# The second half of the first token tile's first row block, loaded by SP's queue instead of ScalarE's

## The chip, the cores and the metric

The kernel runs on one core of a Trainium2 chip. A core has five engines with instruction streams of their own: TensorE (PE in the profile, with its weight loads as PEld), VectorE (DVE), ScalarE (ACT), GpSimd (POOL) and SyncE (SP). SP does no arithmetic here; it issues nearly all DMA transfers. ScalarE issues two of them, at the very start. The transfers of both are carried out by the core's 16 DMA engines.

The metric is the device time of one execution, in microseconds (us), as the median of several runs. The profile is that of one execution.

## The reference

Two branches work on the same tokens `x` (2048 tokens of 448 numbers, float32), and a gate mixes them:

```python
x = A_x
g = _sigmoid((x * gate_w).sum(-1, keepdims=True))
a = _A_ref(x, A_wqkv, A_wo)           # local attention: 16 heads of 28, 8 keys, every second position back
b = _B_ref(x, B_w1, B_b1, B_w2, B_b2) # relu(x @ w1 + b1) ** 2 @ w2 + b2, with 1792 hidden numbers
return g * a + (1 - g) * b
```

In the attention branch `x @ wqkv` gives queries, keys and values. Each query meets the keys at its own position and at 2, 4, ... 14 positions before it. The result is multiplied by `wo`.

## The kernel before, in words

All matrix products are made to float32 accuracy from parts: a matrix is split into a high part (rounded to the type that TensorE multiplies) and a low part (what is left), and a product is high x high, high x low and low x high. So each weight and each token block needs a copy by ScalarE (the high part) and a subtraction by VectorE (the low part) before TensorE can use it.

The 2048 tokens are four chunks of 512 (`CH`), stored transposed: 448 rows of features, 512 columns of tokens. The 448 rows are three row blocks of 128 (k = 0, 1, 2) and a last one of 64, which stands twice, so that two matmuls of 64 rows can run side by side. A chunk's first work is queries, keys and values: for each of its four token tiles of 128 tokens a matmul per row block and part. After all four chunks follow the dense branch's products and the output product, while the attention's elementwise work runs on GpSimd, VectorE and ScalarE.

From line 811 on the order of the work on ScalarE, VectorE and SP comes from a planner (`Plan`), which keeps an estimate of each engine's time. Everything around this change stands before that, in the opening (lines 763 to 808), whose order is written out by hand:

- 18 matmuls on zeros (line 771) keep TensorE busy until data comes.
- ScalarE's queue loads the first token block (k = 0) of chunk 0 in two halves of 256 columns (line 778). The first half holds token tiles 0 and 1, the second half tiles 2 and 3.
- SP's queue loads, for k = 0, 1, 2, the weights of the queries (line 781; 128 rows of 450 numbers, 448 of the queries and two of the gate), with the tokens of the row block behind them (line 786). For k = 0 there are only weights, since the tokens come by ScalarE's queue. For k = 3 the weights are two pieces of 64 rows (line 784). Then follow the weights of keys and values (lines 790 and 793), and later the next chunks' tokens (line 617).
- ScalarE copies the high part of each row block's weights (line 796) and of its tokens (line 799); for the first half it is VectorE that copies (line 801). VectorE subtracts for the low parts: weights on line 803, tokens on line 804. Both engines work strictly in this order.

TensorE's first real work is `qkv_first`, on line 402: for row block 0 first tiles 0 and 1, then tiles 2 and 3, each with three parts; then row blocks 1 and 2 with all four tiles:

```python
for k in range(3):
    todo = [full(x, q[i], i, 0, (k,)) for i in four]
    for some in ((0, 1), (2, 3)) if k == 0 else (four,):
        for j in range(3):
            for i in some:
                acc, a, w, *_ = todo[i][j]
                nc.tensor.matmul(acc.pt[:, :NQ], a, w, start=k == j == 0, stop=False)
```

That makes 3 x 4 x 3 = 36 matmuls. Behind them come the paired matmuls of line 315 (`side_by_side`), which make up the rest of the kernel but for its last stretch.

Of the kernel before, what the change touches and what calls it, by code (L numbers as in the profile page):

```python
# [22 lines left out]
CH = 512  # L23
# [155 lines left out]
def gated_mix_kernel(ctx: ExitStack, tc: tile.TileContext, xT, wqkv, w1, w2, wo, b1, b2, out):  # L179
    nc = tc.nc  # L180
# [593 lines left out]
    raws = [rawp.tile([P, 4, 512], F32, tag="raw", name="wqraw0")]  # L774
    rx = rawp.tile([P, 4, 512], F32, tag="raw", name="xraw0")
    halves = slice(0, 256), slice(256, CH)
    for cols in halves:
        nc.scalar.dma_start(rx[:, 0, cols], xT[0, :, 0, cols])
    for k in range(4):
        if k < 3:  # L780
            nc.sync.dma_start(raws[0][:, k, :NQ], wqkv[0, :, k])
        else:
            for b, rows in ((0, slice(0, 64)), (1, slice(64, P))):
                nc.sync.dma_start(raws[0][rows, k, :NQ], wqkv[b, rows, k])
        if k:
            nc.sync.dma_start(rx[:, k], xT[0, :, k])
    for b, tag in ((1, "k"), (2, "v")):
        raw = attp.tile([P, 3, D], F32, tag=tag, name=f"wqraw{b}")
        for k in range(3):
# [516 lines left out]
```

## Time and profile before

| | us |
|---|---|
| median of 3 runs | 416.2 (415.88 to 416.37) |
| the profiled execution | 415.95 |
| its span, from the first to the last instruction | 414.1 |
| busy in the span: TensorE | 408.6 |
| busy: VectorE / ScalarE / GpSimd | 258.6 / 206.0 / 265.8 |

The profile's times count from the first instruction of the span. A row of a timeline gives the start, the length, the engine (with a q for its sequencer, as where it issues a DMA), the line, the operation, what it writes and reads, how many such instructions were merged, and in brackets the idle time of the engine before it with what ended it. Where several were merged, the length reaches from the first one's start to the last one's end. Matmuls overlap, so a matmul's length is longer than the distance to the next; the distance of the starts is the pace. In the names, `wqraw` holds raw weights of queries, keys and values, `xraw` raw tokens, `wqh` and `wql` the weights' high and low parts, `x` the parts of the tokens.

### The profile page before, as it was taken

The page shows a single profiled execution, that of the slowest core. Times are in us where ns is not written, and L with a number is a line of the kernel's source. Part 1 is how long each engine was busy: PE and PEld are TensorE (multiplying, and loading weights), DVE is VectorE, ACT ScalarE, POOL GpSimd, SP SyncE. Part 2 cuts the span into 40 slices and gives each one's busy share as a digit, 9 for nine tenths or more (in the row PEclk, how much of TensorE's full clock was granted, in tenths as well). Part 3 has the DMA queues.
Part 4 walks back from the last instruction along what each step waited for, and adds up shares of the span by engine and source line. Part 5 has one row for each costly group of instructions (what it writes and reads, how often), then busy time and mean ns, then how long its engine had stood idle before and what let it go on. Part 6 is the DMA issues. An engine that isn't in the chain of part 4 may idle for free.

```text
span 414.1 us, 9249 instructions
## 1 busy us (share of the span) xinstructions
PE 408.6 (99%) x3828; PEld 404.2 (98%) x3828; DVE 258.6 (62%) x346; ACT 206.0 (50%) x501; POOL 265.8 (64%) x165
## 2 busy tenths in 40 slices
PE   8999999999999999999999999999999999999996
PEld 7999999999999999999999999999999999999995
DVE  4514523484386768777656899786767586593453
ACT  5746766242464665444555435345615344346730
POOL 0000000876969999889999897999998975950000
PEclk9999999999999999999999999999999999999999
DMA  7999999845164433544203669663626022068404
GB/s 242 377 346 295 398 378 372 309 156 205 46 215 188 150 106 132 208 161 152 82 4 127 223 149 310 218 162 64 218 91 232 4 90 85 22 158 157 112 2 178
DMA packets 64555, 73.75 MB, mean 178 GB/s; under 512 B 32321, under 2 KB 57345, under 8 KB 64129
## 3 DMA queue, kind: packets, MB, share of 16 engines
q1 hardware_dynamic: 64224, 72.90, 53.5%
q8 instruction: 30, 0.49, 0.5%
q10 hardware_dynamic: 288, 0.26, 0.2%
q14 instruction: 13, 0.10, 0.1%
HBM read 45.71 MB, written 28.25 MB: 179 GB/s over the span
## 4 chain that ended last, share of the span: by engine, by line
PE 98%; DMA 1%; DVE 0%; ACT 0%; issue 0%
PE b L315 32%; PE h L315 32%; PE qkv L315 23%; PE a L315 7%; PE qkv L402 2%; PE a L1096 1%; DMA wqraw<-wqkv 1%; DVE bt_b L987 0%; ACT wqh L796 0%
## 5 line engine op out<-in xcount | busy, mean ns | idle before, releaser
L504 POOL TENSOR_TENSOR pp<-q,k 128x896 f32<-128x896 f32 x64 | 135.1, 2152 | 86.9 <-DMA k<-k_d 78.4
L516 POOL TENSOR_TENSOR pp<-lg,v 128x896 f32<-128x896 f32 x64 | 118.9, 1962 | 4.3 <-DVE lg L508 2.6
L315 PE MATMUL qkv<-wqh,x 64*128 64x448 f32 (+1 forms) x528 | 91.6, 362 | 0.0
L757 DVE TENSOR_TENSOR h<-h,h 128x512 fp32r<-128x512 f32 x56 | 38.7, 691 | 67.2 <-ACT h L756 66.8
L315 PE MATMUL b<-w2ah,h 64*128 64x448 f32 x448 | 78.8, 359 | 0.0
L315 PE MATMUL b<-w2bh,h 64*128 64x448 f32 x448 | 78.7, 359 | 0.0
L508 DVE TENSOR_REDUCE lg<-pp 128x32 f32<-128x896 f32 x64 | 67.5, 1077 | 14.0 <-POOL pp L504 14.0
L315 PE MATMUL qkv<-wql,x 64*128 64x448 f32 (+1 forms) x264 | 75.2, 362 | 0.0
L315 PEld LDWEIGHTS qkv<-wqh,x 64*128 64x128 f32 x528 | 74.0, 184 | 0.3
L526 DVE TENSOR_REDUCE o<-pp 128x112 f32<-128x896 f32 x64 | 67.2, 1069 | 3.1 <-POOL pp L516 3.1
L315 PEld LDWEIGHTS b<-w2ah,h 64*128 64x128 f32 x448 | 63.8, 184 | 0.0
L315 PEld LDWEIGHTS b<-w2bh,h 64*128 64x128 f32 x448 | 62.9, 184 | 0.2
L315 PE MATMUL b<-w2al,h 64*128 64x448 f32 x224 | 63.1, 358 | 0.0
L315 PE MATMUL b<-w2bl,h 64*128 64x448 f32 x224 | 62.3, 358 | 0.0
L753 ACT ACTIVATE h<-h,b1z 128x512 f32<-128x512 f32 x56 | 36.7, 656 | 41.1 <-PE h L315 41.1
L315 PEld LDWEIGHTS qkv<-wql,x 64*128 64x128 f32 x264 | 44.7, 184 | 0.2
L315 PEld LDWEIGHTS b<-w2al,h 64*128 64x128 f32 x224 | 38.4, 184 | 0.0
L315 PEld LDWEIGHTS b<-w2bl,h 64*128 64x128 f32 x224 | 37.7, 184 | 0.1
L315 PE MATMUL h<-x,w1h 64*128 64x512 f32 x168 | 35.7, 386 | 0.0
L315 PE MATMUL h<-x0b,w1h 64*128 64x512 f32 x168 | 35.6, 386 | 0.0
L337 ACT ACTIVATE st<-qkv 128x448 f32<-128x448 f32 x48 | 24.4, 541 | 21.8 <-PE qkv L315 15.8
L755 ACT ACTIVATE h<-h 128x512 fp32r<-128x512 f32 x56 | 33.5, 598 | 1.5
(132 smaller groups left out, 855.6 us busy)
## 6 DMA issues: line engine op xcount, KB each, us to landing
k<-k_d SPq DMA_DIRECT2D x8, 840.0 KB, 6.1
v<-v_d SPq DMA_DIRECT2D x8, 840.0 KB, 4.7
x_d<-x SPq DMA_DIRECT2D x12, 512.0 KB, 6.4
q_d<-st SPq DMA_DIRECT2D x8, 448.0 KB, 4.8
k_d<-st SPq DMA_DIRECT2D x8, 448.0 KB, 4.7
v_d<-st SPq DMA_DIRECT2D x8, 448.0 KB, 5.5
q<-q_d SPq DMA_DIRECT2D x8, 448.0 KB, 3.3
o_d<-o SPq DMA_DIRECT2D x16, 224.0 KB, 2.2
```

The lines of the kernel that those rows point to most:

```text
L315: nc.tensor.matmul(acc.pt[:, :acc.n], a[rows], w[rows], start=acc.todo == acc.all, stop=acc.todo == 1)
L337: nc.scalar.activation(st[0][:, :, t % 2], pt[:, :D].rearrange("p (g c) -> p g c", g=G), AF.Copy)
L402: nc.tensor.matmul(acc.pt[:, :NQ], a, w, start=k == j == 0, stop=False)
L504: nc.gpsimd.tensor_mul(pr.rearrange("p (w c) -> p w c", w=W), q[:, s:s + 1].to_broadcast([P, W, C]), k[:, s:s + W])
L508: nc.vector.tensor_reduce(lgs[i][:, s], pr.rearrange("p (w h d) -> p w h d", w=W, h=HG), axis=AX.X, op=ALU.add)
L516: nc.gpsimd.tensor_mul(pr.rearrange("p (h d w) -> p w h d", h=HG, w=W), lgs[i][:, s][:, :, :, None].to_broadcast([P, W, HG, DH]), vs[i][:, ...
L526: nc.vector.tensor_reduce(o_t[par, s][:, g * C:(g + 1) * C], pr.rearrange("p (c w) -> p c w", w=W), axis=AX.X, op=ALU.add)
L753: a = add(ACT, 656.0, lambda pt=pt, r=r: nc.scalar.activation(pt, pt, AF.Relu, bias=b1t[:, f + r:f + r + 1]), ready, bias_job[0], prio=NEXT)
L755: b = add(ACT, 600.0, lambda pt=pt, hh=hh: nc.scalar.activation(hh, pt, AF.Square), a, prio=NEXT)
L757: low = add(DVE, 690.0, lambda pt=pt, hh=hh, hl=hl: nc.vector.tensor_sub(hl, pt, f32(hh)), a, prio=NEXT)
L1096: nc.tensor.matmul(acc.pt[:, :D], a, w, start=False, stop=acc.todo == 1)
```

## The change

For row block 0, the second half of the tokens (columns 256 to 511) is no longer loaded by ScalarE's queue. SP's queue loads it, right behind the first weights and ahead of the second weights. The first half stays with ScalarE's queue. The loads, their sizes and their destinations are the same; the number of DMA instructions is the same, one less on ScalarE and one more on SP. Nothing is changed in the copies, the subtractions or the matmuls.

```diff
     halves = slice(0, 256), slice(256, CH)
-    for cols in halves:
-        nc.scalar.dma_start(rx[:, 0, cols], xT[0, :, 0, cols])
+    nc.scalar.dma_start(rx[:, 0, halves[0]], xT[0, :, 0, halves[0]])
     for k in range(4):
         if k < 3:
             nc.sync.dma_start(raws[0][:, k, :NQ], wqkv[0, :, k])
         else:
             for b, rows in ((0, slice(0, 64)), (1, slice(64, P))):
                 nc.sync.dma_start(raws[0][rows, k, :NQ], wqkv[b, rows, k])
-        if k:
-            nc.sync.dma_start(rx[:, k], xT[0, :, k])
+        cols = slice(0, CH) if k else halves[1]
+        nc.sync.dma_start(rx[:, k, cols], xT[0, :, k, cols])
```

## The prediction

> **What bounds the kernel now.** I read the page first, then the chain of work that ended last, then the opening by engine. On the page:
>
> ```profile
> span 414.1 us, 9249 instructions
> PE 98%; DMA 1%; DVE 0%; ACT 0%; issue 0%
> ```
>
> The second line gives shares of the chain: TensorE carries 98% of it. The chain's first 14 us (start, length, what) and the busy times of one long stretch (TensorE, its weight loads, VectorE, ScalarE, GpSimd, clock, DMA share, GB/s):
>
> ```profile
> 0.74 3.60 DMA wqraw<-wqkv
> ...
> 4.37 0.59 ACT wqh L796
> ...
> 5.00 7.99 PE qkv L402 x36
> ...
> 13.00:406.00 393.00, 393.00 (x3756) 390.87 (x3756) 248.85 (x327) 198.75 (x489) 264.99 (x152) 1.00 0.53 175
> ```
>
> From 13 us to 406 us TensorE is busy for 393.00 of 393.00 us at clock 1.00. So whatever the opening gains or loses is handed on to the end one for one, and no change to the opening's loads can do more than move the moment at which this stretch begins. Before it stand 36 matmuls of line 402 in 7.99 us. How many of those us are waiting is seen in the timelines of TensorE (PE), and of its weight loads (PEld):
>
> ```profile
> 5.66 0.68 PE L402 MATMUL qkv<-wql,x 128*128 128x450 f32 x2
> 6.18 1.21 PE L402 MATMUL qkv<-wqh,x 128*128 128x450 f32 x4
> 7.23 0.56 PE L402 MATMUL qkv<-wql,x 128*128 128x450 f32 x2
> 7.63 1.36 PE L402 MATMUL qkv<-wqh,x 128*128 128x450 f32 x6
> 6.70 0.30 PEld L402 LDWEIGHTS qkv<-wqh,x 128*128 128x128 f32 x2 [0.33 <-ACT x L799]
> ```
>
> From 7.23 to 7.63 two matmuls start 0.20 us apart; that is the undisturbed pace. 36 of them need 7.20 us, so the stage holds 7.99 - 7.20 = 0.79 us of stalls. One of these belongs to the change: between 6.18 and 7.23 four matmuls took 1.05 us instead of 0.80. Its weight load, at 6.70, waited for ScalarE's copy on line 799, which is the copy of the second half of the tokens. **That stall costs 1.05 - 0.80 = 0.25 us**, the wait and the slow restart after it together. The other stalls (0.54 us) stand before it, at the first weights and their low part.
>
> Why that copy is late, ScalarE and VectorE show (the bracket is the idle time before and what ended it):
>
> ```profile
> 1.67 1.28 ACT L796 ACT_TABLE_LOAD   x1 [1.67 <-PEq L1298]
> 4.37 0.58 ACT L796 ACTIVATE wqh<-wqraw 128x450 fp32r<-128x450 f32 x1 [1.42 <-DMA wqraw<-wqkv]
> 6.23 0.42 ACT L799 ACTIVATE x<-xraw 128x256 fp32r<-128x256 f32 x1 [1.28 <-DMA xraw<-xT]
> 6.55 0.56 ACT L796 ACTIVATE wqh<-wqraw 128x450 fp32r<-128x450 f32 x1
> 7.02 0.61 ACT L799 ACTIVATE x<-xraw 128x512 fp32r<-128x512 f32 x1
> 7.65 0.58 ACT L796 ACTIVATE wqh<-wqraw 128x450 fp32r<-128x450 f32 x1
> 8.58 0.63 ACT L799 ACTIVATE x<-xraw 128x512 fp32r<-128x512 f32 x1 [0.34 <-DMA xraw<-xT]
> 4.54 0.29 DVE L801 CAST x<-xraw 128x256 fp32r<-128x256 f32 x1 [3.54 <-DMA xraw<-xT]
> 4.98 0.63 DVE L803 TENSOR_TENSOR wql<-wqraw,wqh 128x450 fp32r<-128x450 f32 x1
> 5.52 0.42 DVE L804 TENSOR_TENSOR x<-xraw,x 128x256 fp32r<-128x256 f32 x1
> ```
>
> ScalarE stood idle for 1.28 us, until the second half landed at about 6.2. The first half had landed at 4.5, the first weights at 4.34.
>
> **The change, part by part.** The issues of the two queues, SP's waits, and the landings of two later loads (the last number, from issue):
>
> ```profile
> 0.74 0.90 ACTq L778 DMA_DIRECT2D xraw<-xT  x2
> 0.74 0.86 SPq L781 DMA_DIRECT2D wqraw<-wqkv  x2
> 1.65 0.43 SPq L786 DMA_DIRECT2D xraw<-xT  x1
> 2.13 0.43 SPq L781 DMA_DIRECT2D wqraw<-wqkv  x1
> 3.08 1.94 SPq L784 DMA_DIRECT2D wqraw<-wqkv  x2
> 6.22 3.21 SPq L790 DMA_DIRECT2D wqraw<-wqkv  x6
> SPq L784 <- DMA xraw<-xT: 0.9, 1, 0.9
> wqraw<-wqkv SPq DMA_DIRECT2D x1, 225.0 KB, 4.8
> xraw<-xT SPq DMA_DIRECT2D x1, 256.0 KB, 5.0
> ```
>
> *ScalarE loses one DMA issue* (0.90/2 = 0.45 us). Its table load begins about 0.45 earlier, at 1.2. Worth nothing: 1.42 us of idle time follow it, ended by the first weights.
>
> *SP gains one issue*, behind the first weights and ahead of six others of its own: second weights, second tokens, third weights, third tokens and the two pieces on line 784. Each is issued some 0.43 later, up to the second piece. That one waits 0.9 us for the first half (it comes to issue at 4.53, beside VectorE's cast of that half at 4.54), so the delay ends there: 0.43 of the 0.9 us is used up, and everything behind is not later. Whether the delay of the others shows depends on whether the transfers wait for their issue. The packets (q1 is SP's queue, q10 ScalarE's; shares are of 16 engines) in 1.7 to 3.5 us, 3.5 to 5 us, and the total line of 5 to 6.2 us:
>
> ```profile
> DMA packets 258, 0.35 MB, mean 195 GB/s; under 512 B 16, under 2 KB 258, under 8 KB 258
> ...
> q1 hardware_dynamic: 143, 0.24, 54.7%
> q10 hardware_dynamic: 115, 0.11, 21.4%
> q1 hardware_dynamic: 188, 0.31, 58.0%
> q10 hardware_dynamic: 169, 0.15, 38.9%
> DMA packets 266, 0.45 MB, mean 375 GB/s; under 512 B 31, under 2 KB 152, under 8 KB 266
> ```
>
> The two queues take turns, packet by packet (143 against 115, then 188 against 169), and from 3.5 us the engines are 97% taken. A load of 128 rows is 128 packets (0.24 MB in 143 packets is 1.7 KB each, near a row of 450 floats), so eight for each of 16 engines. By 3.5 us the first weights are through and the first half nearly (115 of 128), so the second weights were issued at about 1.2 and moved from about 3.5: over 2 us of cover for 0.43 us of delay. Costed at nothing; without the cover it would be 0.43 us on each landing.
>
> *The first half and the first weights* hold the first place of their queues before and after, and share the engines as before. Their landings, and so the first matmul at 5.00, I leave where they are. Bounds: nothing; or 0.12 us earlier, as ScalarE's copy could begin sooner but VectorE's cast ends at 4.54 + 0.29 = 4.83, against 4.95 of the copy.
>
> *The second half* took its turns on q10 against the second weights (4.8 us from 1.19, landing 5.99) and landed at 6.2, after them. On SP's queue it stands ahead of them, and q10 is empty once the first half is through. A packet of q10 costs 38.9% x 1.5 us x 16 / 169 = 0.055 us, so eight take 0.44 us: landing at 4.52 (just ahead of VectorE's cast of the first half) + 0.44, about **5.0**. Bounds: with the first half (4.5), or not at all earlier (6.2). I take 5.0, since the packet price comes from this very load. ScalarE is free at 4.95, so its copy runs from 5.0 to 5.45, beside idle time. TensorE wants the result at 6.38 + 0.20 = 6.58 at the new pace; the cover is 1.1 us, and even a landing at 6.1 would do. VectorE's low part of the half follows at 5.52 + 0.42 = 5.94 and is done at 6.4; it is wanted four matmuls after 6.58, at 7.38. **The stall of 0.25 us goes.**
>
> *The second weights* now come after the half. The same bytes are through by then as before at 6.2, so they land between 5.8 and 6.2; ScalarE's copy, which before ran at 6.55 behind the half's, starts at 6.0 to 6.2. The second tokens (1.65 + 5.0, landing near 6.65) have the same bytes ahead of them as before. Their copy starts at 6.7 instead of 7.02 and ends at 7.3.
>
> *What is late next.* The second block's first matmul, at 7.63 + 2 x 0.20 = 8.03 before, is wanted at 7.78: 0.47 us after the 7.3. The third weights (copy at 7.65) and third tokens (copy 8.58 to 9.21, set by their landing) are wanted 12 matmuls later, at 10.18. Nothing there takes the place of the stall.
>
> *The loads of line 790* wait for the landings, one by one: the first, at 6.22, stands right behind the half's landing. It can go out about half a us earlier, once the third tokens are issued behind the wait of line 784, and the next ones up to 0.5 us earlier. They queue behind all that the opening needs.
>
> **The sum:** -0.25 us, all else nothing. The profiled execution took 415.95 us round its span of 414.1; the median of the runs is 416.2. So 415.70 for such an execution, and **415.95** against the median.
>
> A rule that speaks against this: the Trainium skill, "DMA: Bandwidth & Descriptors", section "Issuing engines are not separate DMA queues", says that DMAs from several engines run on the same 16 engines and interleave, and that issuing from several at once saves only the sequencer's issue time. By that alone the half would land no sooner, and SP would pay the 0.43 us. The same page, section "Queues, rings and completion order", has the engines take turns between queues and each ring go in order; by that the half comes before the second weights, and the sum is the -0.25 above; by the first it would be nothing, the first rival below. The turns of q1 and q10 above agree with the latter; no run here yet shows which decides for the landing.
>
> **The rivals.**
>
> *The half lands no sooner.* It shares the engines anyhow, and they were full until 6.2. The stall stays where it is: 416.2. For it speaks the 97%; against it, that the second weights landed ahead of the half (5.99) and would now have to stand behind it in their own queue.
>
> *The second block becomes late (slower).* If the half's time adds to q1 in full and the delay of issue as well, the second tokens land 0.44 + 0.43 later, at 7.55; their copy ends at 7.58 + 0.61 = 8.19, and the second block starts at about 8.24 instead of 8.03: +0.2, 416.4. It decides from a landing at about 7.1 on (7.78 less 0.61 and the handing over), and turns the gain to a loss beyond 7.35. Against it: the engines are full, so q10's empty turns go to q1.
>
> *The first matmul moves too (faster).* From 1.7 to 3.5 us the engines moved 195 GB/s, later 375. If the second ScalarE load has to do with that, the first weights and half (225 KB and 128 x 256 floats, 361 thousand bytes) could land up to 361/195 - 361/375 = 1.85 - 0.96 = 0.9 us earlier. Then 0.9 + 0.25 is gained at the most, 415.1; half of it gives 415.5. Against it: the half's packets come only after the first half's, so they can't slow what stands before them.
>
> **How the numbers follow.** Forecast 0.63, half no sooner 0.14, second block late 0.11, first matmul earlier 0.12. About 0.2% (0.83 us) is what a measurement of this kernel can tell from no change; its three runs lie 0.49 us apart. The forecast and the first two rivals lie within that. Of the third, most of the upper end is beyond it: faster 0.10, with a little for the forecast with a larger gain, 0.13 in all. Slower by that much wants the second tokens at 8.2, 1.5 us later: 0.04. Range: 415.95 with the runs' half spread (0.25) is 415.7 to 416.2; it reaches to the slow rival with its spread above (416.7) and below to half of the fast rival's gain, with most of the spread (415.3).
>
> **What would show it.** In the changed profile: one issue on line 778; ScalarE's 128x256 copy near 5.0, not 6.23; four matmuls from about 6.18 in 0.80 us; the second block from 7.78; the long stretch from 12.7. Wrong if the copy still waits until 6, if a weight load waits at the second block, or if the first matmul isn't at 5.0.

## The result, and the profile after

| | us |
|---|---|
| after: median of 12 runs | 416.72 (416.29 to 417.49) |
| before, in the same comparison: median of 12 runs | 415.88 (415.63 to 416.63) |
| ratio after / before | 1.0018, 95% interval 1.0010 to 1.0027 |
| the profiled execution of after | 417.19, span 415.3 |

The changed kernel is slower by 0.84 us, 0.2%. The prediction said 0.25 us faster, 415.95, with 416.7 as the upper end: the sign is wrong, and the time lies just beyond the range. The median of the first three runs of before was 416.2, a little above the 415.88 here; comparisons below are all against before in the same set of runs.

The chain of work that ended last, of the kernel after (start, length, what), with the span and TensorE's share of the chain from the page:

```profile
span 415.3 us, 9249 instructions
PE 97%; DMA 1%; SPq 0%; DVE 0%; ACT 0%; issue 0%
...
2.13 5.89 DMA xraw<-xT
8.05 0.64 ACT x L798
8.73 5.08 PE qkv L402 x24
...
406.98 3.83 PE a L1095 x18
410.83 0.68 DVE bt_b L986
```

The chain no longer runs through the first weights. It starts with the DMA issued at 2.13, and lands 5.89 later, at 8.02. That load is the second tokens (row block 1), not the half that was moved. Block 1 starts at 8.73, where before it started at 8.03, and the last matmuls start at 406.98. Before, the row that answers to this one was:

```profile
406.16 3.83 PE a L1096 x18
```

So TensorE is 0.82 us late at the end. The long stretch in between has not changed, as the stretch of the same 393.00 us shows (columns as in the prediction):

```profile
13.81:406.81 393.00, 393.00 (x3756) 391.21 (x3756) 245.50 (x328) 198.79 (x489) 266.86 (x152) 1.00 0.54 175
```

That makes 0.82 us in the opening. The span is longer by 415.3 - 414.1 = 1.2 us, so another 0.4 us were lost behind the last matmul: from its end to the end of the span it was 414.1 - (406.16 + 3.83) = 4.1 us before and 415.3 - (406.98 + 3.83) = 4.5 us after. The prediction did not look there at all. This execution is one of the slower ones of after (417.19 against a median of 416.72), so it is the 1.2 us of the spans that these terms explain, not the 0.84 us of the medians.

The opening by engine, after. First SP's issues, then ScalarE, then TensorE (columns as in the prediction):

```profile
0.75 0.39 SPq L780 DMA_DIRECT2D wqraw<-wqkv  x1
1.20 0.42 SPq L785 DMA_DIRECT2D xraw<-xT  x1
1.66 0.43 SPq L780 DMA_DIRECT2D wqraw<-wqkv  x1
2.13 0.43 SPq L785 DMA_DIRECT2D xraw<-xT  x1
3.55 1.42 SPq L783 DMA_DIRECT2D wqraw<-wqkv  x2
```

```profile
4.24 0.58 ACT L795 ACTIVATE wqh<-wqraw 128x450 fp32r<-128x450 f32 x1 [1.76 <-DMA wqraw<-wqkv]
4.92 0.42 ACT L798 ACTIVATE x<-xraw 128x256 fp32r<-128x256 f32 x1
5.98 0.58 ACT L795 ACTIVATE wqh<-wqraw 128x450 fp32r<-128x450 f32 x1 [0.65 <-DMA wqraw<-wqkv]
8.05 0.63 ACT L798 ACTIVATE x<-xraw 128x512 fp32r<-128x512 f32 x1 [1.49 <-DMA xraw<-xT]
```

```profile
1.06 4.21 PE L771 MATMUL warm<-zero 128*128 128x256 f32 x18 [1.06 <-DVE b1z L768]
5.07 0.96 PE L402 MATMUL qkv<-wqh,x 128*128 128x450 f32 x2
5.82 0.95 PE L402 MATMUL qkv<-wql,x 128*128 128x450 f32 x2
6.57 1.17 PE L402 MATMUL qkv<-wqh,x 128*128 128x450 f32 x4
7.58 0.56 PE L402 MATMUL qkv<-wql,x 128*128 128x450 f32 x2
7.98 0.56 PE L402 MATMUL qkv<-wqh,x 128*128 128x450 f32 x2
8.73 1.08 PE L402 MATMUL qkv<-wqh,x 128*128 128x450 f32 x4 [0.19 <-ACT x L798]
9.65 0.96 PE L402 MATMUL qkv<-wql,x 128*128 128x450 f32 x4
```

The moved half did what was foretold: its copy starts at 4.92 (6.23 before), the weights' copy behind it at 5.98 (6.55 before). But the next copy, of the second tokens, waits 1.49 us for its DMA and starts at 8.05 (7.02 before). And TensorE itself is slower at the start: the first eight matmuls of line 402 take 7.58 - 5.07 = 2.51 us, where before it was 7.23 - 5.00 = 2.23 us with the stall in it. The warm-up row shows the same: 18 matmuls in 4.21 us, against 3.66 us in the profile of before. The 0.82 us thus consist of 0.35 (block 1 could have started at 7.98 + 2 x 0.20 = 8.38 instead of 8.03: pace), 0.35 (from 8.38 to 8.73: waiting for the tokens) and 0.12 (four matmuls in 9.65 - 8.73 = 0.92 us after the wait instead of 0.80).

The DMA engines from 4 to 6 us, before and after (start:end, length, busy time of TensorE, weight loads, VectorE, ScalarE, GpSimd, then clock, DMA share, GB/s):

```profile
4.00:6.00 2.00, 1.72 (x10) 1.11 (x10) 1.26 (x3) 0.58 (x1) 0.00 (x0) 1.00 0.99 332
```

```profile
4.00:6.00 2.00, 2.00 (x9) 1.87 (x9) 1.45 (x4) 1.01 (x3) 0.00 (x0) 1.00 0.84 264
```

And the queues from 3.5 to 5 us, after (packets, MB, share of 16 engines); before, q10 had 169 packets and 38.9% here:

```profile
q1 hardware_dynamic: 249, 0.33, 78.0%
q10 hardware_dynamic: 15, 0.01, 1.9%
```

With q10 nearly empty, less was moved in all: from 4 to 6 us 332 GB/s became 264. That gives the first of three suspects: the rate of a single queue, the later issue of the second tokens (2.13 instead of 1.65), and whatever happens at the end.

### The profile page after: what moved, and what is told of

Read it like the earlier page. It is cut to its first block, busy times and chain, and to the rows that moved or that the text cites. A ratio compares the mean times of both kernels' runs of the same rounds, so it can differ in the third digit from the quotient of the medians.

```text
span 415.3 us, 9249 instructions
## 1 busy us (share of the span) xinstructions
PE 409.5 (99%) x3828; PEld 405.8 (98%) x3828; DVE 255.0 (61%) x346; ACT 206.3 (50%) x501; POOL 267.7 (64%) x165
## 4 chain that ended last, share of the span: by engine, by line
PE 97%; DMA 1%; SPq 0%; DVE 0%; ACT 0%; issue 0%
PE b L315 32%; PE h L315 32%; PE qkv L315 23%; PE a L315 7%; DMA xraw<-xT 1%; PE qkv L402 1%; PE a L1095 1%; SPq L780 0%; DVE bt_b L986 0%; ACT x L798 0%; SPq L785 0%
## 5 line engine op out<-in xcount | busy, mean ns | idle before, releaser
L504 POOL TENSOR_TENSOR pp<-q,k 128x896 f32<-128x896 f32 x64 | 137.2, 2190 | 89.0 <-DMA k<-k_d 80.6
L315 PE MATMUL b<-w2ah,h 64*128 64x448 f32 x448 | 82.2, 359 | 0.0
L315 PE MATMUL b<-w2bh,h 64*128 64x448 f32 x448 | 82.0, 359 | 0.0
L315 PE MATMUL b<-w2al,h 64*128 64x448 f32 x224 | 70.2, 358 | 0.0
L315 PE MATMUL b<-w2bl,h 64*128 64x448 f32 x224 | 69.1, 358 | 0.0
L315 PEld LDWEIGHTS b<-w2ah,h 64*128 64x128 f32 x448 | 67.1, 184 | 0.0
L315 PEld LDWEIGHTS b<-w2bh,h 64*128 64x128 f32 x448 | 65.7, 184 | 0.2
L315 PEld LDWEIGHTS b<-w2al,h 64*128 64x128 f32 x224 | 41.0, 184 | 0.0
L315 PEld LDWEIGHTS b<-w2bl,h 64*128 64x128 f32 x224 | 40.1, 184 | 0.1
L315 PE MATMUL h<-x1b,w1h 64*128 64x512 f32 x168 | 35.2, 386 | 0.0
```

Source lines behind the costliest of these rows:

```text
L315: nc.tensor.matmul(acc.pt[:, :acc.n], a[rows], w[rows], start=acc.todo == acc.all, stop=acc.todo == 1)
L504: nc.gpsimd.tensor_mul(pr.rearrange("p (w c) -> p w c", w=W), q[:, s:s + 1].to_broadcast([P, W, C]), k[:, s:s + W])
```

## The experiments

All runs come in three sets; within each, before was run beside them (28, 33 and 33 runs; medians 415.96, 415.85 and 415.76). None of these 94 runs, nor of the 12 above, exceeds 416.63.

**The changed kernel once more** (no edit).

> The changed kernel once more, for a second profile. Theory 'one ring': with the second half in SP's queue, ScalarE's queue is empty from about 4 us on, one queue alone feeds the DMA engines less well, and the second tokens land late again, near 8.0 us (6.65 before), so that the second block of matmuls starts near 8.7 and not at 8.03: about +0.7 us against the kernel before. Theory 'chance': the late landing and the late full clock belong to the one profiled execution; the second tokens land anywhere between 6.6 and 8.0, and the time is within 0.3 us of the kernel before.

Measured: 416.66 (415.88 to 417.51), ratio 1.0018 (1.0008 to 1.0027). The slowdown is repeatable. Its profile is another case, though, of the chain's last part and of ScalarE's copy of the second tokens:

```profile
406.49 3.83 PE a L1095 x18
```

```profile
6.64 0.63 ACT L798 ACTIVATE x<-xraw 128x512 fp32r<-128x512 f32 x1
```

Here the tokens landed in time, at 6.62, and the end of the matmuls is late by 0.33 us only, from the pace. So the late landing happens in some executions and not in others. One profile of a kernel is not enough to price this opening.

**Second tokens on ScalarE's queue**, behind the first half. SP has as many DMAs as before again, and both queues have work.

```diff
     nc.scalar.dma_start(rx[:, 0, halves[0]], xT[0, :, 0, halves[0]])
+    nc.scalar.dma_start(rx[:, 1], xT[0, :, 1])
...
-        nc.sync.dma_start(rx[:, k, cols], xT[0, :, k, cols])
+        if k != 1:
+            nc.sync.dma_start(rx[:, k, cols], xT[0, :, k, cols])
```

> The changed kernel, but with the tokens of the second row block (256 KB, 128 packets) issued by ScalarE's queue behind the first half, so that both queues are fed until past 5 us. Theory 'one ring': the second tokens land before 6.2, the second half still near 5, the second block of matmuls starts near 7.8, and the time is 0.2 to 0.3 us under the kernel before. Theory 'issue slot' (SP's extra 0.43 us of issue makes the later loads late): the same, as SP's issues are back in their old places; the run separates both of these from 'chance', which expects no change from the changed kernel.

Measured: 415.88 (415.49 to 416.45), ratio 0.9998 (0.9989 to 1.0007). The whole loss is gone, and nothing is gained either, where two of the theories had expected 0.2 to 0.3 us less than before. From 4 to 6 us the engines moved 352 GB/s:

```profile
4.00:6.00 2.00, 1.66 (x9) 1.09 (x9) 1.26 (x3) 1.00 (x2) 0.00 (x0) 1.00 0.98 352
```

**One issue more on SP in the opening, without the moved half**: the kernel before, with 16 x 4 bytes loaded into a place that a later load overwrites, behind the first weights. Nothing of the computation changes.

```diff
             nc.sync.dma_start(raws[0][:, k, :NQ], wqkv[0, :, k])
+            if k == 0:
+                nc.sync.dma_start(rx[0:16, 3, 0:1], xT[0, 0:16, 3, 0:1])
```

> The kernel before, with one tiny transfer more in SP's queue behind the first weights (16 rows of 4 bytes, overwritten later), which takes an issue slot of about 0.43 us and moves nothing to speak of; both halves stay in ScalarE's queue. Theory 'issue slot': the second tokens land 0.4 us or more later than 6.65 and the time rises by 0.3 to 0.7 us. Theory 'one ring': the landing stays within 0.2 us and the time within 0.3 us.

Measured: 416.69 (416.33 to 417.10), ratio 1.0015 (1.0006 to 1.0024). A DMA of 64 bytes costs nearly as much as the change. Yet its second tokens, issued at 2.11 like those of after, were copied at 6.80:

```profile
6.80 0.63 ACT L801 ACTIVATE x<-xraw 128x512 fp32r<-128x512 f32 x1 [0.66 <-DMA xraw<-xT]
```

So in this execution the later issue alone did not make them late: the theory "issue slot" has the time about right and the landing wrong, "one ring" the other way round. Nor is a queue that works alone slow here. ScalarE's queue was empty from 4.4 us on, and SP's queue by itself moved 320 GB/s (the stretch from 4.5 to 6 us, and the only queue with packets in it):

```profile
4.50:6.00 1.50, 1.50 (x7) 1.34 (x7) 1.37 (x4) 1.23 (x3) 0.00 (x0) 1.00 0.92 320
q1 hardware_dynamic: 278, 0.48, 92.2%
```

In its profile the last matmuls start at 406.54 (0.38 us late, the warm-up matmuls took 4.21 us) and the stretch behind them is 414.8 - (406.54 + 3.83) = 4.4 us long. That brought the end of the program under suspicion: SP has more instructions here, as in after, and the run above, which has not, lost nothing.

**Everything of the opening on SP's queue**: in the kernel after, the first half too.

```diff
-    nc.scalar.dma_start(rx[:, 0, halves[0]], xT[0, :, 0, halves[0]])
+    nc.sync.dma_start(rx[:, 0, halves[0]], xT[0, :, 0, halves[0]])
```

> The changed kernel with the first half in SP's queue too, ahead of the first weights; ScalarE's queue carries nothing. Theory 'one ring': the rate from 2 to 6 us falls below the changed kernel's (230 and 264 GB/s), the first weights land later than 4.3, and the time rises by 0.5 us or more over the changed kernel. Theory 'issue slot': the first weights and all behind come 0.43 us later, at the same rate: about +0.4 over the changed kernel. 'Chance': within 0.45 us of the changed kernel.

Measured: 417.15 (416.39 to 417.67, 6 runs), ratio 1.0026 (1.0014 to 1.0037), the slowest of all. 261 GB/s from 4 to 6 us, and the second tokens' copy at 7.16.

**The change without the extra instruction on SP**: a load of biases at about 60 us, far from any bound, is issued by ScalarE, so that SP has as many instructions as before, while the opening stays that of after. This was run in two sets.

```diff
-    bj = [dma(lambda: nc.sync.dma_start(b1t, b1), 128, 56, prio=LAST, at=60000.0),
+    bj = [dma(lambda: nc.scalar.dma_start(b1t, b1), 128, 56, prio=LAST, at=60000.0),
```

> The changed kernel, with the small bias load at about 60 us (7 KB) issued by ScalarE instead of SP, so that SP's program has as many instructions as in the kernel before; the opening is that of the change. Theory 'end of SP's program' (one instruction more on SP puts a pause of about 0.35 us between its last instructions, at the exit): the stretch from the last matmul to the end of the span is 4.1 us again, not 4.5, and the time falls by 0.4 us from the changed kernel's 416.7, to about 416.3; what is left over the kernel before is the opening's. Theory 'opening alone': the time stays at 416.6 to 416.8.

> The changed kernel with the bias load on ScalarE once more, for the share of late runs (3 of 11 over 417.0 the first time). 'One ring' and 'issue' both: again 2 to 5 runs of 11 over 416.9, the others near 415.8. 'Chance of that call': none or one.

Measured: 415.91 (415.60 to 417.24), ratio 1.0006 (0.9996 to 1.0017); and again 416.40 (415.84 to 417.16), ratio 1.0016 (1.0007 to 1.0025). The two medians differ by half a us, because the runs scatter: 5 of the 22 lie above 416.9, where before has none. The two profiled executions took 417.24 and 416.88, the first as long as any of its eleven; so they show the late case, not the usual one. Chain, span and second tokens' copy of the first:

```profile
core 0 of [0], span 415.5 us
407.52 3.83 PE a L1095 x18
```

```profile
8.57 0.63 ACT L798 ACTIVATE x<-xraw 128x512 fp32r<-128x512 f32 x1 [2.03 <-DMA xraw<-xT]
```

and of the second:

```profile
core 0 of [0], span 415.1 us
407.17 3.83 PE a L1095 x18
```

```profile
8.23 0.63 ACT L798 ACTIVATE x<-xraw 128x512 fp32r<-128x512 f32 x1 [1.58 <-DMA xraw<-xT]
```

Two things follow. The stretch behind the matmuls is back at 415.5 - 411.35 = 4.1 and 415.1 - 411.00 = 4.1 us, with SP's instructions back at their number. And the late tokens of the opening remain (copies at 8.57 and 8.23, with 256 and 226 GB/s from 4 to 6 us): the two losses are separate.

**The extra instruction on SP without the change**: the kernel before, with one, five or seven 4-byte loads more at 60 us, into a place that is not used.

```diff
-    bj = [dma(lambda: nc.sync.dma_start(b1t, b1), 128, 56, prio=LAST, at=60000.0),
+    def bias_load():
+        nc.sync.dma_start(b1t, b1)
+        for p in range(1):  # 5 and 7 in the others
+            nc.sync.dma_start(b1z[p:p + 1, 14:15], b1[p:p + 1, 0:1])
+
+    bj = [dma(bias_load, 128, 56, prio=LAST, at=60000.0),
```

> The kernel before, with one load of 4 bytes more in SP's queue at about 60 us, which nobody reads; the opening is untouched. Theory 'end of SP's program': the stretch from the last matmul to the end is 4.5 us and the time 416.4, 0.4 over the kernel before. Theory 'opening alone': no change, 416.0.

> The same with five such loads. Theory 'end of SP's program', with the pause at a fixed place of the program: the pause moves to the instruction that waits for the last output anyway, and is hidden; the stretch is 3.8 to 4.1 us, the time 0.0 to 0.3 us under the kernel before. If each instruction of SP simply costs at the exit, the stretch is 4.5 or more and the time 416.4 or more. 'Opening alone': 416.0.

> The kernel before with seven late loads of 4 bytes. With one such load the pause stood before SP's last but one instruction of that group, with five it stood right behind the wait for the last output; so with seven it should fall into that wait. Theory 'end of SP's program, fixed place': the stretch from the last matmul to the end is 4.1 us or less instead of 4.41 (five) and 4.45 (one), and the time 0.3 us below these runs, about 415.8. 'Each instruction costs': 4.45 or more, 416.2 or more.

Measured: 416.10, 416.14 and 416.14; ratios 1.0009 (1.0000 to 1.0017), 1.0009 (1.0000 to 1.0018), 1.0007 (0.9998 to 1.0015). One instruction at 60 us, in a program of 416 us whose bound is TensorE, costs about 0.3 us; six more cost nothing further. Each ratio alone stands at the edge of its interval, but the three agree. The chain and span of the kernel with one show where:

```profile
core 0 of [0], span 414.5 us
406.24 3.83 PE a L1101 x18
```

TensorE ends within 0.1 us of before (406.16), and the stretch behind it is 414.5 - 410.07 = 4.4 us instead of 4.1.

SP's own instruction records show what moves there. In all 14 profiles SP pauses for 0.33 to 0.37 us at the same place of its program, behind the 335th of its recorded instructions. In before, the 335th is the second of two records named DRAIN behind the last output, and GpSimd, whose next record follows that drain, goes on 3.0 us behind the last matmul. With one instruction more ahead of it, in after as in the kernel with one late load, the pause stands before that drain, and GpSimd goes on at 3.4; from there to the end it is 1.1 us in all three. With five, the pause follows the wait for the last output, and costs as much, although it was expected to be hidden.

With seven, it falls into that wait, as was expected, but the time saved is not there: the stretch was 4.4 us again. In that profile an 8 KB packet of the queue that the page calls "instruction" (q14) runs beside the output and ends at 2.61 us behind the last matmul, where the output's packets alone end at 2.33, and SP leaves its wait at 2.92 instead of 2.69. In the kernels with fewer late loads that packet comes behind the output. That it delays the wait is likely, but not tested, and neither is why SP pauses.

**The opening with two queues, and late loads**: second tokens on ScalarE's queue (as above), with five and seven late loads.

> The changed kernel with the second row block's tokens on ScalarE's queue (as in the run with both queues fed) and five late loads of 4 bytes. Theory 'end of SP's program': stretch at the exit as with five loads and the kernel before, the opening with the second half at 5.5; 0.1 to 0.4 us under the kernel before. 'Opening alone': as the run without the five loads, 415.9.

> Both queues fed (second half on SP's, second tokens on ScalarE's queue) and seven late loads. 'Fixed place': 0.3 us below the same with five loads (416.16), so 415.8 or a little less; 'each instruction costs': 416.2 or more.

Measured: 416.16, ratio 1.0009 (1.0000 to 1.0018); and 415.90, ratio 1.0004 (0.9995 to 1.0012). The five cost here what they cost in the kernel before, where one theory had expected 0.1 to 0.4 us less than before. With seven, a gain was looked for and there is none. No kernel tried can be told from before on the fast side.

**Third weights on ScalarE's queue**, in the kernel after. The second tokens stay on SP, issued as late as in after (2.13), with more bytes under way beside them; but both queues have work, and SP has as many instructions as before. If the late issue or the bytes are the cause, the tokens stay late; if it is that SP's queue has all the loads, they don't.

```diff
     nc.scalar.dma_start(rx[:, 0, halves[0]], xT[0, :, 0, halves[0]])
+    nc.scalar.dma_start(raws[0][:, 2, :NQ], wqkv[0, :, 2])
...
-            nc.sync.dma_start(raws[0][:, k, :NQ], wqkv[0, :, k])
+            if k < 2:
+                nc.sync.dma_start(raws[0][:, k, :NQ], wqkv[0, :, k])
```

> The changed kernel with the third weights (225 KB) on ScalarE's queue behind the first half: ScalarE's queue is fed past 5 us, but the second tokens stay in SP's queue and are issued at 2.1 us as in the change (1.65 before). SP has as many instructions as before. Theory 'one ring' (one queue alone, when a few of its packets take long, lets a DMA engine fall behind): no run over 416.9, the second tokens land before 7.3, median 415.7 to 416.2. Theory 'issue' (the second tokens are late because they are issued later): a quarter or more of the runs over 416.9, as in the run with the bias load moved.

Measured: 416.01 (415.81 to 416.54), ratio 1.0006 (0.9998 to 1.0015), none of 11 runs above 416.9. The second tokens took 5.0 us from 2.13, as long as before, with 309 GB/s:

```profile
xraw<-xT SPq DMA_DIRECT2D x1, 256.0 KB, 5.0
```

```profile
4.00:6.00 2.00, 1.74 (x10) 1.14 (x9) 1.31 (x4) 1.00 (x2) 0.00 (x0) 1.00 0.98 309
```

Its TensorE rows also show the predicted gain itself, since here the pace was full from the start of line 402, and so was the half early:

```profile
5.00 0.67 PE L402 MATMUL qkv<-wqh,x 128*128 128x450 f32 x2 [0.26 <-ACT wqh L797]
5.67 0.68 PE L402 MATMUL qkv<-wql,x 128*128 128x450 f32 x2
6.19 0.96 PE L402 MATMUL qkv<-wqh,x 128*128 128x450 f32 x4
6.99 0.56 PE L402 MATMUL qkv<-wql,x 128*128 128x450 f32 x2
```

From 6.19 to 6.99 four matmuls take 0.80 us; the first eight take 1.99 instead of 2.23. Most of it is given back at once: the second tokens, landed at 7.1, come a little late for this pace, and the next six matmuls take 1.36 us, from 7.39 to 8.75, instead of 1.20. By its median this kernel can't be told from the first of the two runs with the bias by ScalarE (both 1.0006). A single landing at 7.1 says little too, since after itself landed these tokens at 6.62 once. The runs say more: of the 22 with a second load on ScalarE's queue (this kernel and the one with the second tokens) none exceeds 416.54, of the 22 with the bias by ScalarE, which have none, five exceed 416.9.

**The profiles beside each other.** The second column tells when the last packet of ScalarE's queue started; from then on SP's queue is alone. Rate, landing and matmul times come from the views quoted above, and the landings at 5.9 and 6.0 from the SP issue that waits for them. Each row is one execution.

| kernel | ScalarE's queue at work until | GB/s, 4 to 6 us | second tokens landed (issue) | 18 warm-up matmuls | wait of block 1 for its tokens | behind the last matmul |
|---|---|---|---|---|---|---|
| before | 5.7 | 332 | 6.7 (1.65) | 3.66 | 0 | 4.1 |
| after | 4.1 | 264 | 8.02 (2.13) | 4.21 | 0.35 | 4.5 |
| after, again | 4.3 | 297 | 6.6 (2.13) | 4.21 | 0 | 4.5 |
| all on SP | never | 261 | 7.1 (2.60) | 4.21 | 0 | 4.5 |
| after, bias by ScalarE | 3.9 | 256 | 8.55 (2.12) | 4.21 | 1.21 | 4.1 |
| the same, again | 3.8 | 226 | 8.2 (2.13) | 4.21 | 0.80 | 4.1 |
| second tokens by ScalarE | 5.6 | 352 | 5.9 | 3.66 | 0 | 4.1 |
| the same with five late loads | 5.7 | 320 | 6.0 | 3.85 | 0.37 | 4.4 |
| third weights by ScalarE | 5.5 | 309 | 7.1 (2.13) | 3.69 | 0.16 with the restart | 4.1 |
| tiny load in the opening | 4.4 | 312 | 6.8 (2.11) | 4.21 | 0 | 4.4 |
| one late load | 5.3 | 334 | 6.3 (1.66) | 4.21 | 0 | 4.4 |

In the five profiles with the half on SP's queue and nothing behind the first half on ScalarE's, the rate is 226 to 297 GB/s, and three of them wait for the tokens' landing. In the other nine it is 309 to 352 (325, 329 and 340 in the three not listed), and of these only the third-weights run waits for that landing, for 0.16 us. (The kernel with the second tokens by ScalarE and five late loads waits 0.37 us for the copy of these tokens, but the tokens were there: ScalarE stood idle for 0.75 us before the copy ahead of it, until the second weights landed at 6.6.)

So the late landing goes with the moved half. It does not follow that one queue alone is slow. In the tiny-load kernel SP's queue is alone from 4.4 us on and moves 320 GB/s; and from 6 us to the end of the opening it is alone in every kernel. In before, from 6 to 7 us:

```profile
6.00:7.00 1.00, 1.00 (x5) 0.67 (x4) 0.32 (x1) 0.77 (x2) 0.00 (x0) 1.00 1.04 382
```

These are loads of the same sizes. What lowers the rate between 4 and 6 us where the half was moved, and not always, stays open.

**The account.** The runs of the changed opening scatter to one side, so means are better than medians for a sum. The change by itself: 416.75 - 415.98 = +0.77, and again 416.74 - 416.04 = +0.70. The extra instruction alone (one, five, seven late loads): +0.34, +0.31, +0.32. The opening alone (the two runs with the bias by ScalarE): +0.29 and +0.66, or 0.47 in the middle; with a second load on ScalarE's queue (second tokens, third weights) -0.12 and +0.23. Together 0.32 + 0.47 = 0.79 us, about what the change costs.

The weak place of this sum is the tiny load in the opening. It costs 0.62 us by its means, of which the end explains about 0.3, and the other 0.3 us come without a moved half and, in its profile, without late tokens; there TensorE is 0.38 us late from the slow pace of its start alone. So a part of the 0.47 us may be due to the extra issue in the opening and not to the late landing.

What else stays open: why the rate is lower where the half was moved (in after the engines show a share of 0.84 from 4 to 6 us instead of 0.99, but no run took that apart); whether the change also shifts the odds of the slow pace of TensorE's start, as it comes in kernels with untouched openings too; and why SP pauses near the end.

## Why the prediction was wrong, point by point

- *The second half lands at about 5.0, its copy at 5.0*: right, 4.92.
- *The stall of 0.25 us goes*: right in mechanism; the third-weights run shows 0.24 (2.23 - 1.99). But it is there to be gained only in an execution where TensorE is at full pace from the first matmul on. The prediction took the pace of one profile (full when line 402 begins) as the kernel's own. In the kernel with five late loads, whose opening is that of before and whose half landed as late, the same four matmuls went from 6.69 to 7.58, in 0.89 us instead of 1.05, and the first one on the half followed its neighbour at 0.21 us, without a stall, since the slow pace had moved the need back:

```profile
6.40 0.42 ACT L799 ACTIVATE x<-xraw 128x256 fp32r<-128x256 f32 x1 [1.43 <-DMA xraw<-xT]
```

```profile
6.69 1.05 PE L402 MATMUL qkv<-wqh,x 128*128 128x450 f32 x4
7.58 0.56 PE L402 MATMUL qkv<-wql,x 128*128 128x450 f32 x2
```

- *The second tokens "have the same bytes ahead of them as before", landing near 6.65*: **this is the step that failed**. The bytes were the same, but not the rate: 264 GB/s instead of 332, a landing at 8.02. The sentence that carried it, "the engines are full, so q10's empty turns go to q1", was held against the slow rival. It says how the turns are shared out, not that the sum of what is moved stays the same, and the sum did not: 297 GB/s and a landing at 6.62 in one execution, 226 to 264 and 8.02 to 8.55 in three. The forecast took a single value for it.
- *The rival "second block becomes late"* had the right place, and its points of decision (7.1 for a wait, 7.35 for a loss) hold for full pace; the waiting executions landed at 8.02 to 8.55. Its size was too small: it added 0.44 and 0.43 us to 6.65 for 7.55. Of its two causes the later issue does not by itself make these tokens late (issued at 2.11 and 2.13, they landed at 6.8 with the tiny load and at 7.1 with the third weights on ScalarE's queue).
- *SP's extra issue, "costed at nothing"*: **this term was wrong too**. It costs some 0.3 us behind the last matmul, in a stretch of 4.1 us that the prediction never looked at; in the opening the price is not settled (the tiny load there leaves some 0.3 us unexplained). That the number of DMAs stays the same was not the point; SP has one more.
- *The rules weighed*: by the first of the two the half would land no sooner, but it landed sooner: its copy ran at 4.92 instead of 6.23, ahead of the second weights' at 5.98, as the order within a queue has it. That first rule, in the Trainium skill, "DMA: Bandwidth & Descriptors", section "Issuing engines are not separate DMA queues", has issuing from several engines save only the sequencer's time. On the rates the runs do not decide. In the third-weights run the second tokens are issued by SP at the same moment as in after, and with a second queue at work 309 GB/s are moved instead of 264; but with the tiny load SP's queue alone moved 320.
- *The first matmul stays at 5.00*: 5.07, close enough. *First matmul earlier*, the fast rival, did not happen: 219 GB/s from 1.7 to 3.5 us, against 195.
- *Slower by over 0.2% wants the second tokens at 8.2, chance 0.04*: the profiled execution landed them at 8.02, and the kernel is 0.84 us slower. But one of the two losses came from outside the sum; the chance was taken from the opening alone.

## What to carry to other kernels

When a load moves to another queue, do not take the landing of what stands behind it as one value: the moved half put the second tokens anywhere from 6.6 to 8.5 us. Giving the emptied queue another load in exchange removed the late runs here, though the cause was not found. An instruction added to SP can have a price at the end of the program as well as at its place, so add up the stretch behind the last matmul as a term of its own, and look where SP pauses in it. A gain read from the opening of one profile should be checked against a second one, since pace and landings differ there from one execution to the next.

## What the runs showed of the hardware that was not expected

- With the half on SP's queue and no second load on ScalarE's, 226 to 297 GB/s were moved from 4 to 6 us, in the other kernels 309 to 352; and the landing of one load of 256 KB issued at 2.13 scattered from 6.6 to 8.5 us. A queue alone is not slow as such: SP's moved 382 GB/s from 6 to 7 us in before, and 320 from 4.5 to 6 us with the tiny load.
- The stretch from the end of the last matmuls to the end of the span was 4.1 us in each of the five profiles with SP's number of instructions as before, and 4.3 to 4.5 us in each of the nine with one to seven more, wherever these were issued. SP pauses for 0.33 to 0.37 us behind its 335th recorded instruction in all 14, so one instruction more decides which of its last steps the pause stands before.
- The 18 warm-up matmuls took 3.66 to 3.85 us in four profiles and 4.21 in ten, though these matmuls are the same in all kernels, and in the latter the slow pace went on into line 402 (four matmuls in 1.50 us from 5.07 to 6.57 in after), while the granted clock reads 1.00. The Trainium skill, "TensorE: Matmul & The Clock Gate", Part 1, tells of a free-running window by which the warm-up varies from run to run; these profiles agree with the variation, and do not show the window.
